# A Fourier mixing layer feeding eight experts: one half store ahead of the sums of weights, the last two batches' early stages 1 to 2 blocks sooner, and the second product of seven from block 40

## The chip, the cores and the metric

The kernel runs on one core of one Trainium2 chip. A core has a matrix engine (TensorE, "PE" in the profile, with its weight loads as "PEld"), VectorE ("DVE"), ScalarE ("ACT"), GpSimd ("POOL") and SyncE ("SP"), which run at the same time and wait for each other through semaphores. Transfers between the chip's memory and the core are issued by SyncE, ScalarE and GpSimd and share 16 DMA engines. The metric is the device time of one execution in microseconds, as the median of several runs.

## The reference

```python
# 1: mixing, per batch and channel: x is (8, 2496, 256)
X = np.fft.rfft(x, axis=1)
Y = X * (filt_r + 1j * filt_i)[None]
x = np.fft.irfft(Y, n=2496, axis=1).reshape(19968, 256)
# 2: each token goes to one of 8 experts by a hash of its id
expert_idx = token_ids * np.int64(2654435761) % np.int64(8)
for e in range(8):                       # w1: (8, 256, 1024), w2: (8, 1024, 256)
    mask = expert_idx == e
    out[mask] = np.maximum(x[mask] @ w1[e], 0.0) @ w2[e]
```

All data are float32.

## The kernel before

**The transform.** A batch of 2496 positions is treated as 39 by 64. `stage1` multiplies with a table of the short transform, and its results go out to a table `d` in the chip's memory. `load2` reads them back turned (`mid<-d` in the profile, L306). `forward` is the second product (`pb`), followed on VectorE by the multiplication with the filter: a product `y`, two halves of a product `z`, and their sum (L321, L325, L326). `back` is the way back (`pc`, L338), written to memory again; `load4` reads it (L409), and `stage3` makes the result (`pd`). The result rows go by indirect transfers of GpSimd (`scatter`, L436) to `xs`, sorted by expert. A full piece of stage 3 issues four such transfers.

**The experts.** `xs` is cut into tiles of 256 tokens of one expert. The main loop takes one tile per step; a step is called a block below, and there are 80 of them that are always needed, numbered from 0. A block has two matrix products, `x @ w1` (`up`) and `h @ w2` (`down`). `up` is made by Strassen's scheme: seven products of halves in place of eight, each of four 128x128x128 matmuls (in float32 each shows as two records). For it, `token_parts` turns the tokens (L861), `token_sums` makes four sums of quarters of the tokens on VectorE (L874), and `weight_sums` makes four sums of quarters of `w1` on GpSimd (L883, tiles `tw`), one block ahead. Inside `up`, VectorE adds products up out of the matrix engine's result memory (L900), and ScalarE applies the relu (L897).

**Early and late blocks.** In blocks below `WS` (L54), `down` is a plain product of 16 matmuls of 256 columns (L928). From block `WS` on, `late_step` calls `both`, where `down` too is made of seven products (L955). This needs sums of quarters of `w2`. They are made once for each expert by `prepare` (loads L211, four subtractions on GpSimd L199, a write to memory L218), and are loaded with each change of expert into the space of the tables `d_t` and `e_t` (L472). These tables and the filter, whose space holds the tokens' sums in late blocks, are needed by `forward` and `back` until batch 7 has passed them. So `WS` cannot come before the end of batch 7's stage 2.

**The order.** All engines take their instructions in the order in which the program issues them. That order is written out by hand: a list `todo` holds the pieces of batches 2 to 7 with a due time in units of blocks, and `run_until` issues what is due at six places of a block: after `up`, after each of the first three quarters of `down`, and at its end. `batch(b, t1, t2, t3)` spreads six pieces of stage 1 over the interval t1, ten of `forward` and `back` over t2, and six of stage 3 over t3; loads are issued up to 2.5 blocks ahead. `within` moves each piece into the second half of its block.

**Weights and stores.** `weights(i, 0)` and `weights(i, 1)` load `w1` (L467) and `w2` (L470) of block i two blocks ahead, on SyncE's queue, and only where the expert changes; there are two buffers. The result of block i is copied to `osb` (L933) and written by `store`, two indirect transfers of GpSimd, one for each half of 128 tokens (L1021). In an early step the order on GpSimd is: four sums of the next block's weights, both half stores of the block before, and then the scatters of the pieces that fall into the block. In a late step it is: the second half store, the four sums, the first half store.

**Stages of tiles.** Tiles that hold only tokens of the first batches come first: the tiles from block 50 on need all eight batches.

Of the kernel before, what the change touches and what calls it, by code (L numbers as in the profile page):

```python
# [50 lines left out]
NPAD = NT * TB - N  # L51
NQP = NPAD // P
NSURE = NT - 5
WS = 42  # L54

# [68 lines left out]
def kernel(  # L126
# [76 lines left out]
    def prepare(e, part):  # L203

        if part == 0:
            p = t4pool if e < 4 else xpool
            raw[e] = p.tile([P, FP, C], F32, name=f"raw_{e}", tag="t4" if e < 4 else "x")
            w = raw[e][:].rearrange("p k c -> p (k c)").rearrange("p (k f c) -> p k f c", k=4, c=P)
            src = moe_w2[e].rearrange("(fp p) c -> p fp c", p=P)
            for k, (f, c) in enumerate(((0, 0), (1, 1), (0, 1), (1, 0))):  # L210
                nc.sync.dma_start(out=w[:, k], in_=src[:, 4 * f:4 * f + 4, P * c:P * c + P])  # L211
        elif part < 5:
            w = raw[e][:].rearrange("p k c -> p (k c)").rearrange("p (k f c) -> p k f c", k=4, c=P)
            to, p, q = ((0, 2, 0), (2, 1, 2), (1, 1, 0), (3, 3, 1))[part - 1]
            minus(nc.gpsimd, w[:, to], w[:, p], w[:, q])
        else:
            w = raw[e][:].rearrange("p k c -> p (k c)").rearrange("p (k n) -> p k n", k=4)
            nc.sync.dma_start(out=t2_dram[e].rearrange("p (k n) -> p k n", k=4), in_=w)  # L218
# [230 lines left out]
    def weights(i, which):  # L449
# [19 lines left out]
        else:  # L469
            eng.dma_start(out=ws[i][1], in_=moe_w2[bass.ds(e, 1)].rearrange("one (fp p) d -> p (one fp) d", p=P), **kw)  # L470
            if WS <= i < NSURE:
                eng.dma_start(out=late["t2"][i % 2].rearrange("p k f c -> p (k f c)"),  # L472
                              in_=t2_dram[bass.ds(e, 1)].rearrange("one p k -> p (one k)"), **(kw if i >= WS + 2 else {}))

# [251 lines left out]
    def spaced(t0, t1, n):  # L726
        return [t0 + (t1 - t0) * u / n for u in range(n)]

    def within(todo, share=.5):

        return [(t // 1 + .5 + t % 1 * share, piece) for t, piece in todo if t is not None]

    def part1(b, at, loads):
        bt = batches[b]
        return within([(at[u], lambda u=u: bt.stage1(u)) for u in range(NU)] +
                      [(loads[v], lambda v=v: bt.load1(v)) for v in range(NV)])

    def part2(b, at, loads, lag):
        bt = batches[b]
        return (within([(at[u], lambda u=u: bt.forward(u)) for u in range(NS // 2)], .3) +  # L740
                within([(at[u] + lag, lambda u=u: bt.back(u)) for u in range(NS // 2)] +
                       [(loads[g], lambda g=g: bt.load2(g)) for g in range(NS // SG)]))

    def part3(b, at, loads):
        bt = batches[b]
        return within([(at[u], lambda u=u: bt.stage3(u)) for u in range(NU)] +
                      [(loads[v], lambda v=v: bt.load4(v)) for v in range(NV)])
# [53 lines left out]
    todo = [(t - 200, piece) for t, piece in head]  # L801
    todo += [(t, lambda k=k: pads(k)) for k, t in enumerate((10.9, 11.6, 11.9, 16.9, 17.6, 17.95, 22.9))]

    def batch(b, t1, t2, t3):

        a1, a2, a3 = spaced(*t1, NU), spaced(*t2, N_2), spaced(*t3, NU)
        x0, d0, e0 = t1[0] - 2.5, t2[0] - 1.2, t3[0] - 1.2
        out = part2(b, a2, [max(d0, a2[2 * g] - 2.2) for g in range(NS // SG)], .6)
        out += part3(b, a3, [max(e0, a3[2 * v] - 2.2) for v in range(NV)])
        if b > 2:  # L810
            out += part1(b, a1, [max(x0, a1[2 * v] - 2.5) for v in range(NV)])
        return out
# [5 lines left out]
    todo += part2(3, spaced(6.4, 10, N_2), [5.2, 5.4, 5.6, 6.5, 7.5], .6)  # L818
    todo += part3(3, spaced(12, 16, NU), [11.2, 11.4, 12.5])
    todo += batch(4, (7.5, 11), (12.4, 16.4), (18.3, 22.3)) + batch(5, (13, 17), (18.4, 21.6), (23.2, 26.8))  # L820
    todo += batch(6, (20, 24), (25.5, 31.5), (33.6, 39.6)) + batch(7, (28.5, 33), (34, 38.8), (40.6, 46.6))
    for e in range(E):
        t = 26.4 + 1.2 * e if e < 4 else 33.4 + 1.3 * (e - 4)
        todo += within([(t + d, lambda e=e, k=k: prepare(e, k)) for k, d in enumerate((0, 1.1, 1.3, 1.5, 1.7, 1.9))])
    todo.sort(key=lambda t: t[0])
    pre = [t for t in todo if t[0] < 0]
# [31 lines left out]
    def token_parts(i, to=None):  # L858

        xt = work.tile([P, DP, 2, P], F32, name=f"xt_{i}", tag="xt")[:] if to is None else to  # L860
        nc.vector.transpose(out=xt.rearrange("p d h (a t) -> p (h a) d t", t=32),  # L861
                            in_=xg[i][:, :, 0:C // 4].rearrange("p a (c d) -> p a d c", d=DP))
        parts[i] = {(h, d): xt[:, d, h, :] for h in range(2) for d in range(DP)}
# [13 lines left out]
    def weight_sums(i, eng=None):  # L877

        eng, w1, h = eng or nc.gpsimd, ws[i][0], F // 2
        b11, b12, b21, b22 = [w1[:, d, f * h:f * h + h] for d in range(DP) for f in range(2)]  # L880
        t = [tpool[i % 2].tile([P, h], F32, name=f"tw_{i}_{k}", tag=f"tw{k}") for k in range(4)]
        for k, (p, q) in enumerate(((b12, b11), (b22, t[0][:]), (b22, b12), (b21, t[1][:]))):
            eng.tensor_tensor(t[k][:], p, q, op=OP.subtract)  # L883
        sums[i] = t

    def up(i, ht, between=lambda: None):
        w1, x, st, t = ws[i][0], parts[i], parts[i]["sums"], sums[i]
        ps = {k: banks[k].tile([P, 4, P], F32, name=f"up_{i}_{k}", tag=k) for k in "abc"}
        h11, h12, h21, h22 = [ht[:, h, 4 * f:4 * f + 4, :] for h in range(2) for f in range(2)]

        def product(bank, w, xx, first, fs=range(4)):
            for f in fs:
                nc.tensor.matmul(out=ps[bank][:, f, :], lhsT=w[:, f * P:(f + 1) * P], rhs=xx,  # L893
                                 start=first and f == 0, stop=True, skip_group_check=True)

        def relu(out, in_):
            nc.scalar.activation(out=out, in_=in_, func=AF.Relu)  # L897

        def plus(out, bank, other):
            nc.vector.tensor_tensor(out, ps[bank][:], other, op=OP.add)  # L900

        h = F // 2
        product("a", w1[:, 0, 0:h], x[0, 0], True)
        nc.scalar.copy(out=h21, in_=ps["a"][:])
        between()
        product("b", t[1], st[:, 1, :], True)
        plus(h12, "b", h21)
        product("c", t[0], st[:, 0, :], True)
        plus(h22, "c", h21)
        product("a", w1[:, 1, 0:h], x[0, 1], False, (0, 1))  # L910
        product("b", t[2], st[:, 2, :], False)
        plus(h22, "b", h22)
        relu(h22, h22)
        product("a", w1[:, 1, 0:h], x[0, 1], False, (2, 3))
        relu(h11, ps["a"][:])
        product("c", w1[:, 1, h:], st[:, 3, :], False)
        plus(h12, "c", h12)
        relu(h12, h12)
        product("b", t[3], x[1, 1], False)
        plus(h21, "b", h21)  # L920
        relu(h21, h21)
# [96 lines left out]
    def store(i, halves=range(2)):  # L1018
        o = rows[i]
        for h in halves:  # L1020
            st = nc.gpsimd.indirect_dma_start(  # L1021
                out=out[:], out_offset=bass.IndirectOffsetOnAxis(ap=to_rows[i][:, h:h + 1], axis=0),
                in_=o[:, h, :], in_offset=None, bounds_check=N - 1, oob_is_err=False)
            tc.declare_no_dep(st.ins, group="out_rows", reason="distinct rows")
            tc.add_to_no_dep_group("out_rows", st.ins)
# [9 lines left out]
    def ask(i, sooner=False):  # L1035

        j = asked[0]
        if j <= i + 2 or (sooner and j == i + 3 < NT and stage_of[j] == stage_of[j - 1]):
            if j < NT:
                load(j)  # L1040
                asked[0] += 1
# [11 lines left out]
    def late_step(i):  # L1053
        ht = work.tile([P, 2, FP, P], F32, name=f"ht_{i}", tag="ht")
        store(i - 1, (1,))
        if i + 1 < NSURE:
            weight_sums(i + 1)
        store(i - 1, (0,))
        both(i, ht)

    def step(i):
        if i >= WS:
            late_step(i)
            return
        ht = work.tile([P, 2, FP, P], F32, name=f"ht_{i}", tag="ht")
        if i + 1 < NSURE:
            weight_sums(i + 1)
        if i > 0:
            store(i - 1)
        up(i, ht, lambda: ask(i))  # L1070
        weights(i + 2, 0)
        if i + 1 < NSURE:
            token_parts(i + 1)
            token_sums(i + 1)
        run_until(i + .6)
        down(i, ht, lambda k: spot(i, k))
        weights(i + 2, 1)
        run_until(i + 1)
# [59 lines left out]
```

## Time and profile before

| | us |
|---|---|
| median of 3 runs (1409.99 to 1411.53) | 1410.83 |
| the profiled execution | 1449.27 |
| its span, from the first to the last instruction | 1447.6 |
| TensorE busy | 1381.2 |
| VectorE busy | 884.7 |
| GpSimd busy | 831.2 |
| ScalarE busy | 418.5 |
| mean granted clock of TensorE, as a share of full speed | 0.984 |

The profiled execution is one run with the hardware profiler on. Its time is 38.4 us above the median of the plain runs. A row of the profile names a line of the kernel, an engine, an operation, and the tile that is written and those that are read; `x8` counts instructions. In a timeline a row has its start and its duration in us, and in brackets how long its engine had been idle before it and what ended that. In a table of stretches each engine has its busy time and, in brackets, its instructions; then follow the clock, the mean busy share of the DMA engines, and the GB/s that they moved. In a list of waits, a row has the time in total, the number of times, and the longest.

### The profile page before, as it was taken

How to read it: one execution, taken by the hardware profiler on the slowest of the kernel's cores; microseconds unless marked ns; L12 is line 12 of the kernel's file. 1: busy time of each engine (PE TensorE's matmuls, PEld its weight loads, DVE VectorE, ACT ScalarE, POOL GpSimd, SP SyncE). 2: the span in 40 equal slices, each digit the busy share in tenths (PEclk: the TensorE clock that was granted, in tenths of full speed). 3: DMA queues.
4: the chain of work that ended last, by engine and by line, in shares of the span. 5: the costliest groups of instructions: out<-in, count | busy, mean ns of one | idle time of the engine just before them, and what ended most of it. 6: DMA issues, size and time to landing. Idle time of an engine off the chain costs nothing.

```text
span 1447.6 us, 26942 instructions
## 1 busy us (share of the span) xinstructions
PE 1381.2 (95%) x9618; PEld 1282.0 (89%) x9618; DVE 884.7 (61%) x1708; ACT 418.5 (29%) x776; POOL 831.2 (57%) x736
## 2 busy tenths in 40 slices
PE   7887999899999989999999999999999999999997
PEld 7775888788888878888899988999999999999997
DVE  6673485465466446534765577456776667677775
ACT  4543222232223222323222222222222222222222
POOL 6155342753475464557766378777565555555663
PEclk9998999999999999999999999999999999999999
DMA  8675765658897597698997876766662616161611
GB/s 221 203 239 182 197 206 144 193 192 257 264 263 251 161 292 225 216 280 258 292 298 219 234 225 214 202 221 194 219 190 48 212 45 215 40 212 45 215 46 34
DMA packets 253949, 284.67 MB, mean 197 GB/s; under 512 B 125651, under 2 KB 222342, under 8 KB 243620
## 3 DMA queue, kind: packets, MB, share of 16 engines
q1 hardware_dynamic: 104589, 185.62, 41.0%
q10 hardware_dynamic: 129303, 52.69, 15.2%
q0 software_dynamic: 19920, 44.59, 8.9%
q8 instruction: 79, 1.29, 0.4%
q14 instruction: 58, 0.48, 0.1%
HBM read 302.04 MB, written 86.15 MB: 268 GB/s over the span
## 4 chain that ended last, share of the span: by engine, by line
PE 83%; DMA 6%; DVE 6%; another core or an unknown queue 2%; issue 1%; ACT 1%; ACTq 0%; SPq 0%; POOLq 0%; DVEq 0%; POOL 0%
PE dps L928 19%; PE up_b L893 8%; PE up_a L893 5%; PE dnc L955 4%; PE pd L270 4%; PE dna L955 4%; PE dnb L955 4%; PE up_c L893 4%; PE upc L950 4%; PE upa L950 4%; PE pb L315 4%; PE pa L270 3%; PE pc L338 3%; DMA xg<-xs 3%; PE upb L950 2%; PE dne L955 2%
## 5 line engine op out<-in xcount | busy, mean ns | idle before, releaser
L928 PE MATMUL dps<-wts,ht 128*128 128x256 f32 x1344 | 314.1, 382 | 0.2 <-ACT ht L897 0.2
L436 POOL DMA_INDIRECT xs<-o,sidx x176 | 178.6, 1015 | 212.5 <-ACT o L272 82.7
L1021 POOL DMA_INDIRECT out_dram<-osb,no x158 | 167.0, 1057 | 221.1 <-DVE osb L962 162.5
L928 PEld LDWEIGHTS dps<-wts,ht 128*128 128x128 f32 x1344 | 255.8, 192 | 38.8 <-issue 2.4
L883 POOL TENSOR_TENSOR tw<-wts 128x512 f32<-128x512 f32 x158 | 203.7, 1289 | 87.3 <-DMA wts<-in_moe_w_dram 61.2
L883 POOL TENSOR_TENSOR tw<-wts,tw 128x512 f32<-128x512 f32 x158 | 204.4, 1294 | 6.2
L900 DVE TENSOR_TENSOR ht<-up_b,ht 128x512 f32<-128x512 f32 x126 | 87.1, 691 | 124.2 <-PE up_b L893 69.6
L897 ACT ACTIVATE ht<-ht 128x512 f32<-128x512 f32 x126 | 79.2, 630 | 176.5 <-DVE ht L900 151.2
L325 DVE TENSOR_TENSOR z<-pb,filt 64x512 f32<-64x512 f32 x160 | 110.2, 689 | 27.6 <-PE pc L338 24.2
L959 ACT ACTIVATE ht<-ht 128x512 f32<-128x512 f32 x114 | 71.9, 631 | 154.3 <-DVE ht L962 106.5
L933 DVE COPY osb<-dps 128x512 f32<-128x512 f32 x42 | 29.1, 692 | 127.2 <-PE dps L928 113.8
L893 PE MATMUL up_a<-xt,wts 128*128 128x128 f32 x672 | 96.7, 277 | 4.6 <-issue 1.9
L893 PE MATMUL up_b<-st,tw 128*128 128x128 f32 x672 | 90.7, 278 | 6.7 <-DVE ht L900 5.1
L893 PEld LDWEIGHTS up_a<-xt,wts 128*128 128x128 f32 x672 | 88.7, 192 | 7.8 <-issue 3.3
L893 PEld LDWEIGHTS up_b<-st,tw 128*128 128x128 f32 x672 | 82.5, 193 | 9.0 <-POOL tw L883 5.1
L341 ACT COPY mid<-pc 128x512 f32<-128x512 f32 x60 | 34.9, 582 | 167.2 <-PE pc L338 69.1
L955 PE MATMUL dna<-wts,ht 128*128 128x128 f32 x608 | 80.4, 275 | 0.0
L900 DVE TENSOR_TENSOR ht<-up_c,ht 128x512 f32<-128x512 f32 x84 | 57.9, 689 | 36.0 <-PE up_c L893 22.0
L270 PE MATMUL pd<-t,wi_t 120*117 120x256 f32 x320 | 77.1, 383 | 2.2 <-ACT o L272 1.3
L950 PE MATMUL upa<-filt,wts 128*128 128x128 f32 x592 | 78.2, 275 | 0.0
L315 PE MATMUL pb<-mid,d_t 128*128 128x256 f32 x280 | 74.9, 391 | 3.0 <-DVE z L325 1.9
L321 DVE TENSOR_TENSOR y<-pb,filt 128x512 f32<-128x512 f32 x80 | 55.1, 688 | 36.1 <-PE pb L315 27.6
(209 smaller groups left out, 2613.8 us busy)
## 6 DMA issues: line engine op xcount, KB each, us to landing
wts<-in_moe_w_dram SPq DMA_DIRECT2D x162, 1024.0 KB
xg<-xs ACTq DMA_DIRECT2D x321, 64.0 KB
d_t<-t2s SPq DMA_DIRECT2D x19, 1024.0 KB
e_t<-t2s SPq DMA_DIRECT2D x19, 1024.0 KB
mid<-d SPq DMA_DIRECT2D x70, 256.0 KB
d<-mid ACTq DMA_DIRECT2D x60, 256.0 KB
x<-in_x_dram SPq DMA_DIRECT2D x39, 312.0 KB
t<-d SPq DMA_DIRECT2D x12, 960.0 KB
```

Of the source, the lines that this page charges most:

```text
L270: nc.tensor.matmul(out=ps[0:cols * H, k, :], lhsT=w[:], rhs=src[:, 2 * i + k, :], start=True, stop=True)
L315: nc.tensor.matmul(out=ps[:, i, :], lhsT=d_t[:, s, :], rhs=rhs, start=True, stop=True)
L325: nc.vector.tensor_tensor(out=z[b], in0=ps[a], in1=f_t[1][64 * hi:64 * hi + 64, s1:s1 + 2, :], op=OP.mult)
L436: st = nc.gpsimd.indirect_dma_start(out=xs[:], out_offset=bass.IndirectOffsetOnAxis(ap=index, axis=0), in_=rows, in_offset=None, bounds_ch ...
L883: eng.tensor_tensor(t[k][:], p, q, op=OP.subtract)
L893: nc.tensor.matmul(out=ps[bank][:, f, :], lhsT=w[:, f * P:(f + 1) * P], rhs=xx, start=first and f == 0, stop=True, skip_group_check=True)
L897: nc.scalar.activation(out=out, in_=in_, func=AF.Relu)
L900: nc.vector.tensor_tensor(out, ps[bank][:], other, op=OP.add)
L928: nc.tensor.matmul(out=ps[:, h, :], lhsT=ht[:, h, fp, :], rhs=w2[:, fp, :], start=(fp == 0), stop=(fp == FP - 1))
L950: nc.tensor.matmul(out=ps[:, f, :], lhsT=w[:, f * P:(f + 1) * P], rhs=xx, start=first and f == 0, stop=True, skip_group_check=True)
L955: nc.tensor.matmul(out=ps[:, 0, :], lhsT=a[:, f, :], rhs=b[:, f, :], start=first and f == 0, stop=True, skip_group_check=True)
L1021: st = nc.gpsimd.indirect_dma_start(out=out[:], out_offset=bass.IndirectOffsetOnAxis(ap=to_rows[i][:, h:h + 1], axis=0), in_=o[:, h, :], i ...
```

## The change

Three edits. `WS` goes from 42 to 40, so that blocks 40 and 41 make their second product of seven too. The due times of batches 6 and 7, and of the preparation of the sums of `w2` of experts 4 to 7, are moved: batch 6's stage 1 half a block earlier, its stage 2 one block earlier and over 5 blocks in place of 6, its stage 3 one block earlier; batch 7's stage 1 and 2 and the preparation two blocks earlier, its stage 3 1.2 blocks earlier. In an early step, the second half store of the block before is issued ahead of the sums of weights, and the first half after them, as in a late step.

```diff
-WS = 42
+WS = 40
...
-    todo += batch(6, (20, 24), (25.5, 31.5), (33.6, 39.6)) + batch(7, (28.5, 33), (34, 38.8), (40.6, 46.6))
+    todo += batch(6, (19.5, 23.5), (24.5, 29.5), (32.6, 38.4)) + batch(7, (26.5, 31), (32, 36.6), (39.4, 45.4))
     for e in range(E):
-        t = 26.4 + 1.2 * e if e < 4 else 33.4 + 1.3 * (e - 4)
+        t = 26.4 + 1.2 * e if e < 4 else 31.4 + 1.3 * (e - 4)
         todo += within([(t + d, lambda e=e, k=k: prepare(e, k)) for k, d in enumerate((0, 1.1, 1.3, 1.5, 1.7, 1.9))])
...
         ht = work.tile([P, 2, FP, P], F32, name=f"ht_{i}", tag="ht")
+        if i > 0:
+            store(i - 1, (1,))
         if i + 1 < NSURE:
             weight_sums(i + 1)
         if i > 0:
-            store(i - 1)
+            store(i - 1, (0,))
```

## The prediction

> **What bounds the kernel now.** I read the page first, then TensorE's waits, then a cut of the span into blocks (a block begins with the first matmul of its first product), then the timeline of two stalls.
>
> ```profile
> span 1447.6 us, 26942 instructions
> PE 1381.2 (95%) x9618; PEld 1282.0 (89%) x9618; DVE 884.7 (61%) x1708; ACT 418.5 (29%) x776; POOL 831.2 (57%) x736
> PE 83%; DMA 6%; DVE 6%; another core or an unknown queue 2%; issue 1%; ACT 1%; ACTq 0%; SPq 0%; POOLq 0%; DVEq 0%; POOL 0%
> ```
>
> TensorE is the bound: 95% busy, 83% of the chain that ended last. Time falls only if TensorE gets less work or stands still less. The cut, with us, busy time per engine, clock, DMA share and GB/s:
>
> ```profile
> 910.00:923.60 13.60, 13.50 (x90) 12.48 (x89) 5.02 (x11) 3.55 (x6) 12.87 (x12) 1.00 0.59 193
> 923.60:938.40 14.80, 14.80 (x97) 13.71 (x96) 5.84 (x12) 4.13 (x7) 7.70 (x8) 1.00 1.03 254
> 938.40:953.90 15.50, 15.16 (x97) 13.87 (x97) 5.79 (x12) 4.04 (x7) 10.91 (x11) 1.00 0.60 172
> 953.90:968.90 15.00, 14.47 (x121) 13.99 (x120) 10.21 (x21) 4.46 (x9) 12.39 (x11) 1.00 0.71 228
> 968.90:983.90 15.00, 14.59 (x122) 14.13 (x122) 9.12 (x21) 4.45 (x9) 12.06 (x12) 1.00 0.74 226
> 983.90:998.60 14.70, 14.48 (x122) 14.02 (x121) 8.85 (x21) 4.45 (x9) 11.46 (x11) 1.00 0.50 144
> 998.60:1012.70 14.10, 14.01 (x119) 13.08 (x119) 9.16 (x22) 4.01 (x9) 9.91 (x9) 1.00 0.83 287
> 1012.70:1025.20 12.50, 12.50 (x115) 12.50 (x114) 8.79 (x20) 3.49 (x7) 7.32 (x6) 1.00 0.89 295
> ```
>
> These are blocks 39 to 46. From 42 on they are late blocks (14 products); 40 to 45 each carry a piece of batch 7's stage 3. A bare late block is 12.50, TensorE never idle. The stalls:
>
> ```profile
> PE up_b L893 <- DVE ht L900: 11.5, 13, 3.8
> PE pa L270 <- issue: 6.0, 2, 3.9
> PE pc L338 <- DVE y L326: 4.9, 2, 3.1
> ```
>
> All small, and none is for a DMA. The 4.9 are one of 3.10 in block 1 and this one in block 3 (214.5 to 236.0):
>
> ```profile
> 220.38 1.27 POOL L883 TENSOR_TENSOR tw<-wts 128x512 f32<-128x512 f32 x1 [2.17 <-DMA wts<-in_moe_w_dram]
> ...
> 223.19 1.24 DVE L874 TENSOR_TENSOR st<-st,xt 128x128 f32<-128x128 f32 x1
> 224.36 1.35 DVE L874 TENSOR_TENSOR st<-xt 128x128 f32<-128x128 f32 x1
> 225.63 0.28 DVE L874 TENSOR_TENSOR st<-xt,st 128x128 f32<-128x128 f32 x1
> ...
> 228.79 0.45 PE L338 MATMUL pc<-y,e_t 128*128 128x256 f32 x1 [1.82 <-DVE y L326]
> ```
>
> GpSimd makes block 5's weight sums as soon as the weights are there, at 220.38 to 225.56, beside VectorE's token sums; those take 1.24 and 1.35 in place of 0.28. VectorE is late, y is late, TensorE waits 1.82. A second kind of stall, in block 24 (from 644.7):
>
> ```profile
> 648.80 0.99 POOL L436 DMA_INDIRECT xs<-o,sidx  x1 [0.30 <-issue]
> 649.81 1.27 POOL L883 TENSOR_TENSOR tw<-wts 128x512 f32<-128x512 f32 x1
> 650.70 0.69 DVE L900 TENSOR_TENSOR ht<-up_b,ht 128x512 f32<-128x512 f32 x1 [2.25 <-PE up_c L893]
> 651.54 0.68 PE L893 MATMUL up_b<-xt,tw 128*128 128x128 f32 x4 [1.32 <-DVE ht L900]
> ```
>
> up_b ended at 648.88, yet VectorE was let go 0.89 after GpSimd went from indirect transfers to sums. I call this a hold: a row of indirect transfers that turns straight into sums. It costs when it falls on an addition with little slack.
>
> **Part 1, blocks 40 and 41 late.** Products of four 128-column matmuls start 0.895 apart; a second product in halves is 16 matmuls of 256 columns, 1.73 for four. Early: 7 x 0.895 + 4 x 1.73 = 13.2. Late: 14 x 0.895 = 12.5. Two blocks: 1.3 less. With the stage-3 pieces I use rows: blocks 39 to 45 now are 13.6 + 14.8 + 15.5 + 15.0 + 15.0 + 14.7 + 14.1 = 102.7. Afterwards the pieces sit one block earlier: block 39 is early with a piece (14.8), 40 to 43 late with one (mean of 15.0, 15.0, 14.7: 14.9 each), 44 the last piece (14.1), 45 bare (12.5): 101.0. **Gain 1.7**, or 1.3 if every late piece costs 15.0. SyncE issues two more 1 MB loads of sums (0.33 each); each has a block of 14.8 to land while TensorE works. If that cover were gone, TensorE would wait for the rest of the landing.
>
> **Part 2, the half store.** It changes GpSimd's order in each early block: half store (1.0, and 0.3 between two), four sums (5.2), half store. Where GpSimd is ahead, the sums can no longer begin in the block before; the store waits for osb (mostly ready 0.9 to 1.2 into the block), so sums run from about 2.4 to 7.6, under additions out of PSUM. Token sums start at 7.8. What waits behind the store is the sums and then the scatters; the sums' reader is TensorE in the next block, at least 4 us after they would end in every early block. In block 3 the 2.6 us of collision go and with them **1.8**. Block 1's 3.10 stays: there the sums wait for the weights till 176.4, store or not. A lone store ahead of sums gives no hold: bare late blocks do just that, without a stall.
> Where GpSimd is behind with scatters, the sums begin 1.3 later. In blocks 15 and 24 they began 4.6 and 5.1 into the block and held the third addition (stalls 0.86 and 1.32); at 5.9 and 6.4 that addition is past: 2.2 gained. In blocks 11, 17, 18, 23 and 26 they began at 3.7 (stalls 0.6, 0, 0.7, 0.1, 0) and move to 5.0, block 24's place: up to 1.3 each, 6.5 together; but block 12 began at 5.1 without a stall, so I take a little over half, 3.6, less the 1.4 that goes. Net 0.0, between -2.2 and +4.3 - 1.4 = +2.9. Token sums lengthen by up to 1.0 in such blocks; behind them y is ready at least 1.9 us ahead of its product in every block from 7 on, so nothing; without that slack it would be 1.0 a block. Block 6's sums follow ten indirect transfers; one place later may add 1.3 to its stall of 3.81; I take **+0.4** as an expectation.
>
> **Part 3, stages sooner.** TensorE's work is only moved. It costs where cover is thin. Batch 6's third load is now asked for at the end of block 19, ahead of the stage-1 piece in block 20 that frees its buffer; SyncE waits with it some 7 us into block 20, with block 21's second and block 22's first weights behind. Block 20 is 31 long and their readers sit 6 us into block 21 or later: 0. Batch 6's stage 2 moves one block, batch 7's stage 1 two blocks, so blocks 23 to 25 (53.2 us, 14.8 MB by the rows below) take about 2.3 MB more.
>
> ```profile
> 626.30:644.70 18.40, 18.29 (x110) 15.80 (x108) 7.26 (x16) 6.12 (x12) 12.93 (x12) 1.00 1.04 315
> 644.70:661.30 16.60, 15.28 (x97) 13.91 (x96) 5.96 (x11) 4.56 (x8) 13.21 (x13) 1.00 0.93 293
> 661.30:679.50 18.20, 17.74 (x109) 16.07 (x109) 8.63 (x17) 5.09 (x9) 13.95 (x14) 1.00 0.73 229
> ```
>
> Here a rule differs from the row. The Trainium skill (DMA: Bandwidth & Descriptors, Specifications) gives about 358 GB/s of HBM per core: 19.0 MB would fit, all of it hidden. The rows show engines full at about 300: 16.0 MB, so 1.1 MB spill, 4 us. By the page 0; by the row 4 us of lateness against leads of 0.7 block (12 us): also 0. Were that lead gone, 4 us of stall. Stage 3 of batch 6 gains room, its first read comes 1.8 blocks after the last back product in place of 0.9. Counted at 5.2 for four sums and 1.3 for each transfer or subtraction, GpSimd has 85 of 92 us to do in blocks 32 to 36 (94 of 106 in 33 to 38 before); I add **+0.4** for that, between 0 and 2.
>
> **Price of a new stall.** The Trainium skill (TensorE: Matmul & The Clock Gate, What's actually happening) halves the clock after an idle window of about 3.4 us; shorter stalls would cost face value. The trace is harsher: block 1's 3.10 is followed by 184.5 to 189.2 at 0.64, block 20's 0.36 + 1.89 by a mean of 0.95 over 31.2 us. 1.82 in block 3 left 1.00. So block 3 is worth 1.8 by both, a new 4 us stall 4 by the page and 5.7 by the rows (3.4 us at half lose 1.7); I use the rows.
>
> **Sum.** -1.7 - 1.8 + 0.0 + 0.4 + 0.4 = -2.7; the profiled execution (1449.3, of it 1447.6 span and 1.7 around it) would become 1446.6. The runs without profile stand at 1410.8, 38.4 shorter; the removed pieces are TensorE time and engine order, so I carry them over whole: **1408.1**.
>
> **Rivals.**
> A. Only TensorE's saving survives: holds arrive in all five blocks, or block 3's stall finds another cause. For it: the four places at exactly 5.0. Against: blocks 5 and 12. -1.7 + 1.2: about 1410.3.
> B. Slower by the hold: one more transfer before the sums lengthens the standstills of block 6 (1.87 + 3.81, clock 0.87) and block 19 (2.40 + 1.84, clock 0.88). Each 1.3 longer may open another half-clock window, 3.0 each; with the five new holds (+5.1) and without the other gains but 1.7, 1410.8 + 9.4 = 1420 at the worst, 1415 at half. It decides once new waits pass 6.3 (the gains of 3.5, and 2.8 for 0.2%). For it: standstills sit at the longest rows of transfers. Against: rows keep their length, only the place of one store changes.
> C. DMA crowding in blocks 23 to 25 makes batch 6's first product late: 4 us and half a clock window, 1408 + 5.7 = 1414. Against: TensorE waits for no DMA at a share of 1.04.
> D. The shift breaks up one standstill of block 6 or 19: 5 to 8 less, 1402.
>
> **How the numbers follow.** Chances: main case 0.44 (own range 1405.5 to 1410), A 0.26, B 0.13, C 0.09, D 0.08. 0.2% (2.8 us) is what a measurement can tell: faster means below 1408.0. The main case lies on that edge and gives 0.28 faster, 0.16 same; D 0.08 faster; A 0.26 same; B 0.12 slower, 0.01 same; C slower. Faster 0.36, same 0.43, slower 0.21. Range 1403 to 1414.5: it leaves out most of D and the upper half of B and C.
>
> **What would show it.** Right: blocks 40 and 41 near 14.9; no wait in block 3; sums beginning about 2.4 into blocks GpSimd is ahead in; stalls gone from 15 and 24. Wrong: new up_b waits at 5 us into blocks 11, 17, 18, 23, 26; longer ones in 6 and 19; pb or pd waiting for a DMA after block 23.

## The result, and the profile after

The changed kernel takes 1428.8 us (1427.2 to 1430.8); the kernel before takes 1410.4 beside it (1408.4 to 1411.5). The ratio is 1.0143, with a 95% interval from 1.0117 to 1.0169: **18.4 us slower**. The forecast was 1408.1, in a range of 1403.0 to 1414.5.

The prediction reads a profile of an execution that is much longer than the plain runs. For what follows, the kernel before was profiled again in an execution of 1406.0; it is called "before, plain" here. The page of after, first its lines that answer to those shown of before:

```profile
span 1425.5 us, 27077 instructions
PE 1371.5 (96%) x9666; PEld 1278.0 (90%) x9666; DVE 936.5 (66%) x1726; ACT 421.3 (30%) x780; POOL 832.6 (58%) x736
```

and those of before, plain:

```profile
span 1404.3 us, 26942 instructions
PE 1365.1 (97%) x9618; PEld 1273.2 (91%) x9618; DVE 908.3 (65%) x1708; ACT 420.8 (30%) x776; POOL 833.7 (59%) x736
```

TensorE is the bound in both. VectorE is 28 us busier. Its sums of tokens in early blocks (L874, tile `st`, three groups in the profile) take 133.7 in place of 102.6, though there are eight fewer. The largest of these groups, in after and then in before, plain (behind the bar: busy us, mean ns of one):

```profile
L874 DVE TENSOR_TENSOR st<-xt 128x128 f32<-128x128 f32 x82 | 73.8, 901 | 1.4
L874 DVE TENSOR_TENSOR st<-xt 128x128 f32<-128x128 f32 x86 | 49.9, 580 | 1.5
```

The two more late blocks add work to VectorE too, and the sums `y<-y,z` take 12.8 less. TensorE's waits in after, the longest of them:

```profile
PE pb L315 <- DMA mid<-d: 4.5, 1, 4.5
PE pb L315 <- issue: 4.4, 2, 3.4
...
PE pd L270 <- DVE z L325: 3.0, 3, 1.6
PE pb L315 <- DVE z L325: 3.0, 2, 1.9
PE pc L338 <- DVE z L325: 2.7, 2, 2.6
...
PE pd L270 <- DMA t<-d: 2.5, 2, 1.9
...
PE pa L270 <- DVE z L325: 2.3, 2, 1.9
```

and the waits of before, plain, behind `z` from block 0 on:

```profile
PE pd L270 <- DVE z L325: 1.8, 2, 0.9
...
PE pc L338 <- DVE z L325: 1.3, 1, 1.3
```

The wait of 4.5 for a transfer (`mid<-d`) is new. The waits behind `z` have grown: from block 0 on, they are 3.1 in before, plain, and 9.9 in after (1.1 of the row of `pb` behind `z` lies ahead of block 0), and most of the 4.4 that end with "issue" will turn out to belong to them. To place all this I cut each trace into blocks and took from each block what its matmuls need at full clock: 13.2 for an early one, 12.5 for a late one, 0.43 for each further 256-column matmul of a piece. The rest is called excess (idle time, and time lost to half clock). Sums by stretch, in us, from one execution of each kernel:

| blocks | before, plain | stages moved only | after | after, sums of tokens late | both repairs |
|---|---|---|---|---|---|
| 0 and 1 | 4.7 | 10.2 | 5.7 | 3.5 | 3.4 |
| 2 to 17 | 8.0 | 8.9 | 6.0 | 8.7 | 11.0 |
| 18 to 21 | 2.8 | 12.8 | **16.9** | 9.9 | 5.6 |
| 22 to 26 | 1.3 | 1.6 | 2.4 | 5.3 | 4.8 |
| 27 to 38 | 4.0 | 8.8 | **13.5** | 4.4 | 5.6 |
| 39 to 45 | 1.6 | 0.3 | 0.3 | 0.3 | 0.3 |
| span | 1404.3 | 1423.2 | 1425.5 | 1410.0 | 1409.3 |

Executions of one kernel differ, so only large differences count: another one of the kernel before, the first of the experiments, has 8.3 in blocks 0 and 1 and 11.6 in 18 to 21. The 10.2 of the stages moved in blocks 0 and 1, where nothing is moved, are such a difference.

The loss lies in blocks 18 to 21 (14.1) and 27 to 38 (9.5). Half of the second part (4.8) is there with the stages moved alone. Where the prediction looked for gains, they came: block 3 is 19.2 and has no wait, and blocks 39 to 45 are at bare time. Blocks 39, 40 and 44 of after, as a table of stretches:

```profile
892.60:907.50 14.90, 14.90 (x98) 13.78 (x97) 5.84 (x12) 4.13 (x7) 9.46 (x9) 1.00 0.76 234
907.50:921.70 14.20, 14.20 (x121) 13.93 (x120) 10.82 (x21) 4.45 (x9) 12.42 (x11) 1.00 0.72 234
...
964.40:978.10 13.70, 13.70 (x118) 12.95 (x117) 9.97 (x21) 4.01 (x9) 10.54 (x9) 1.00 0.48 146
```

Late blocks with a piece are 14.2, with TensorE never idle.

**Block 18: a queue's order.** SyncE's issues (SPq) and the first product they feed, in after (block 17 begins at 470.7, block 18 at 483.8):

```profile
476.73 2.52 SPq L252 DMA_DIRECT2D x<-in_x_dram  x3
479.37 0.47 SPq L409 DMA_DIRECT2D t<-d  x1
484.21 10.60 SPq L306 DMA_DIRECT2D mid<-d  x4
...
496.53 1.71 PE L315 MATMUL pb<-mid,d_t 128*128 128x256 f32 x4 [4.55 <-DMA mid<-d]
```

and in before, plain (block 17 begins at 471.2, block 18 at 484.4):

```profile
477.89 2.54 SPq L306 DMA_DIRECT2D mid<-d  x4
...
492.78 1.03 PE L315 MATMUL pb<-mid,d_t 128*128 128x256 f32 x4
...
494.64 6.61 SPq L252 DMA_DIRECT2D x<-in_x_dram  x3
```

Stage 1 of batch 6 is due half a block sooner, and its first load of `x` with it. That load is now issued in block 17 *ahead* of batch 5's reads `mid<-d`, where before it came behind them. SyncE then stands still before its next reads, as its own waits show (470 to 500):

```profile
SPq L306 <- DMA xg<-xs: 8.3, 1, 8.3
SPq L306 <- DMA x<-in_x_dram: 4.3, 1, 4.3
```

The four reads that were all issued by 480.4 are now strung out to 494.8. TensorE waits 4.55, and its granted clock over the block is 0.93: 6.5 in all.

**Block 28: late on VectorE.** In after (the block begins at 695.3):

```profile
702.71 1.00 POOL L1021 DMA_INDIRECT out_dram<-osb,no  x1 [0.15 <-issue]
...
703.08 3.32 DVE L874 TENSOR_TENSOR st<-xt 128x128 f32<-128x128 f32 x1
703.74 3.85 POOL L199 TENSOR_TENSOR raw<-raw 128x512 f32<-128x512 f32 x3
...
706.43 1.30 DVE L874 TENSOR_TENSOR st<-st,xt 128x128 f32<-128x128 f32 x1
...
708.06 0.68 DVE L321 TENSOR_TENSOR y<-pb,filt 128x512 f32<-128x512 f32 x1
708.75 1.39 DVE L325 TENSOR_TENSOR z<-pb,filt 64x512 f32<-64x512 f32 x2
...
710.24 1.10 PE L315 MATMUL pb<-mid,d_t 128*128 128x256 f32 x4 [3.36 <-issue]
```

The first half's store and the preparation's subtractions follow the sums of weights on GpSimd and meet VectorE's four sums of tokens, which take 5.2 in place of 1.1. The `y` and `z` of a product that TensorE finished at 702.6 are queued behind them. Products of pieces share four buffers of result memory (`fps`). The first `pb`, two `pa` and a `pc` fill them, so the next `pb` starts only when `z` has read the first: 3.36 of standstill, ending 0.1 after `z`. The profile calls its releaser "issue"; the times name it.

**Block 32: a read that lands late.** Not every wait in blocks 27 to 38 is one behind `z`. In after:

```profile
779.03 2.60 PE L270 MATMUL pd<-t,wi_t 120*117 120x256 f32 x8 [1.95 <-DMA t<-d]
```

This is a read of batch 6's stage 3, which the change moved too. With half a clock window behind it, the block has an excess of 3.9; before, plain, has no such wait there. With the stages moved alone the wait is 0.66. Why the read is late was not tested.

### The profile page after: what moved, and what is told of

It is laid out like the page before. It is cut to its first block, busy times and chain, and to the rows that moved or that the text cites. A ratio compares the mean times of both kernels' runs of the same rounds, so it can differ in the third digit from the quotient of the medians.

```text
span 1425.5 us, 27077 instructions
## 1 busy us (share of the span) xinstructions
PE 1371.5 (96%) x9666; PEld 1278.0 (90%) x9666; DVE 936.5 (66%) x1726; ACT 421.3 (30%) x780; POOL 832.6 (58%) x736
## 5 line engine op out<-in xcount | busy, mean ns | idle before, releaser
L928 PE MATMUL dps<-wts,ht 128*128 128x256 f32 x1280 | 297.7, 381 | 0.3 <-ACT ht L897 0.3
L928 PEld LDWEIGHTS dps<-wts,ht 128*128 128x128 f32 x1280 | 243.1, 191 | 36.1 <-issue 2.0
L900 DVE TENSOR_TENSOR ht<-up_b,ht 128x512 f32<-128x512 f32 x120 | 82.9, 691 | 97.7 <-PE up_b L893 72.4
L893 PE MATMUL up_a<-xt,wts 128*128 128x128 f32 x640 | 92.9, 279 | 3.5 <-DVE xt L861 3.3
L893 PE MATMUL up_b<-st,tw 128*128 128x128 f32 x640 | 86.2, 278 | 1.3 <-DVE ht L900 0.5
L955 PE MATMUL dna<-wts,ht 128*128 128x128 f32 x640 | 84.5, 275 | 0.0
L950 PE MATMUL upa<-filt,wts 128*128 128x128 f32 x624 | 82.4, 275 | 0.0
L893 PEld LDWEIGHTS up_b<-st,tw 128*128 128x128 f32 x640 | 78.8, 194 | 3.0 <-issue 2.8
L199 DVE TENSOR_TENSOR filt<-ht 128x512 f32<-128x512 f32 x80 | 61.2, 765 | 27.9 <-ACT ht L959 27.9
L955 PEld LDWEIGHTS dna<-wts,ht 128*128 128x128 f32 x640 | 77.9, 192 | 0.0
```

What stands on the lines that cost most here:

```text
L928: nc.tensor.matmul(out=ps[:, h, :], lhsT=ht[:, h, fp, :], rhs=w2[:, fp, :], start=(fp == 0), stop=(fp == FP - 1))
L950: nc.tensor.matmul(out=ps[:, f, :], lhsT=w[:, f * P:(f + 1) * P], rhs=xx, start=first and f == 0, stop=True, skip_group_check=True)
L955: nc.tensor.matmul(out=ps[:, 0, :], lhsT=a[:, f, :], rhs=b[:, f, :], start=first and f == 0, stop=True, skip_group_check=True)
```

## The experiments

Kernels of one group ran on one chip, beside runs of the kernel before. Ratios are to those, with 95% intervals.

**1. The parts one by one.** First the kernel before again, to have its profile near its plain runs:

> The kernel before, unchanged, to have its profile from an execution whose time is near its plain runs. The profile shown before was of an execution of 1449.3, 38.4 longer than the median. Theory 1 (that execution was disturbed at single places): span about 1409, head some 13 shorter (block 0 begins at about 143 in place of 156), and blocks 1, 6 and 19 some 5 to 8 each shorter; then gains counted from that profile in those places were not there to be had. Theory 2 (the profiler lengthens every execution alike): again about 1447, the same stalls at the same places.

It took 1420.0: between the theories. The head (what runs before block 0) was 11.4 shorter and blocks 6 and 19 were at bare time, but blocks 18 and 20 had 4.1 and 5.7 of excess. The kernel before varies by itself in those blocks.

The half store alone (before, with the last hunk of the change):

```diff
+        if i > 0:
+            store(i - 1, (1,))
         if i + 1 < NSURE:
             weight_sums(i + 1)
         if i > 0:
-            store(i - 1)
+            store(i - 1, (0,))
```

> The kernel before with the half store ahead of the sums of weights in early blocks, and nothing else. Theory H (the half store is what costs: the sums wait for osb, the first half's store and the subtractions of the preparation land on VectorE's sums of tokens in blocks 27 to 33, VectorE is late, and TensorE waits for result memory that VectorE has not read): slower than before by 8 to 15 us. Theory M (the moved stages are what costs): within 2 us of before, or 1.8 faster by block 3 (the prediction's own sum for this part: -1.8 + 0.0 + 0.4).

1408.2 beside 1409.2: ratio 0.9987 (0.9974 to 1.0000). So theory H is wrong: alone, the half store costs nothing that can be measured. It brings 2.3 in block 3 and costs 1.1 in block 15, 1.3 in block 21 and 1.1 in block 34.

The moved stages and preparation alone (`WS` stays 42):

> The kernel before with only the stages of batches 6 and 7 and the preparation moved; late blocks still begin at 42, and both half stores stay behind the sums. Theory M (loads of x for batch 6 go ahead of batch 5's reads of d on SyncE's queue, TensorE waits 4.5 in block 18 and runs at half clock behind it; batch 7's pieces crowd blocks 26 to 33): slower than before by 10 to 18. Theory H: slower by 4 to 8 at most, of it block 18 alone (5.3 over the block's bare time), the rest of the loss then being the half store's. The prediction's sum for this part was +0.4.

1422.2 beside 1409.2: ratio 1.0087 (1.0066 to 1.0108). Theory M holds for this part: block 18's excess is 7.0, blocks 27 to 38 have 4.8 more than before, plain.

The changed kernel without the half store:

> The changed kernel with both half stores behind the sums again, so that stages are moved and late blocks begin at 40. Against the run with the stages moved alone it tells what blocks 40 and 41 bring: 1.3 to 4 less (the prediction: 1.7; the trace after: 4.7 over blocks 39 to 45). Theory H: 2 to 5 slower than before, some 14 faster than the changed kernel. Theory M: as slow as the changed kernel or 2 more (block 3's gain gone), 1428 to 1431.

1421.0: ratio 1.0092 (1.0062 to 1.0122). It lies between the theories. Against the run above, blocks 39 to 45 are 98.0 in place of 99.3: **1.3 for two late blocks**, less than the totals can tell apart. Against the changed kernel (1428.8) the half store costs 7.8, or 7.2 by the two ratios, where alone it cost nothing. The two parts don't add up; they meet somewhere.

**2. The order on SyncE.** The stages moved, but batch 6's loads of `x` due 2.0 blocks ahead:

```diff
-            out += part1(b, a1, [max(x0, a1[2 * v] - 2.5) for v in range(NV)])
+            lead = 2 if b == 6 else 2.5
+            out += part1(b, a1, [a1[2 * v] - lead for v in range(NV)])
```

> The kernel with only the stages moved, but the three loads of x for batch 6 are due 2.0 blocks ahead of their pieces in place of 2.5, so that the first of them is issued behind batch 5's first reads of d on SyncE, as in the kernel before. Stage 1 itself stays half a block sooner. Theory Q (the order on SyncE's queue costs: a wait of 5.0 for mid<-d and 1.7 at half clock in block 18, and what follows in 19 and 20): block 18 back to 18.4, the whole 7 to 10 shorter than the run with the stages moved (1422.2), at 1412 to 1415. Theory P (the pieces crowd blocks 18 to 20, whatever the order of the loads): 1420 or more.

Block 18 fell to 18.9, excess 0.6 in place of 7.0, so the order is the cause of its wait. But the whole was 1418.7, ratio 1.0071 (1.0045 to 1.0096): only some 2 to 3 came through, which these intervals don't tell from nothing. Block 20 shows where 3.0 of it went (excess 6.0 in place of 3.0). Its timeline in this run (the block begins at 527.9; the kernel's lines are one further down):

```profile
535.77 1.27 POOL L884 TENSOR_TENSOR tw<-wts 128x512 f32<-128x512 f32 x1 [2.29 <-DMA wts<-in_moe_w_dram]
536.09 1.10 DVE L875 TENSOR_TENSOR st<-xt 128x128 f32<-128x128 f32 x1
...
537.22 1.32 DVE L875 TENSOR_TENSOR st<-st,xt 128x128 f32<-128x128 f32 x1
...
539.74 1.35 DVE L875 TENSOR_TENSOR st<-xt,st 128x128 f32<-128x128 f32 x1
...
546.16 2.00 PE L315 MATMUL pb<-mid,d_t 128*128 128x256 f32 x4 [1.90 <-DVE z L325]
```

The sums of weights now start at 7.8 into the block, when their weights land, and run beside all four sums of tokens, which take 5.1. In before, plain, where block 20 is short (an excess of 0.5), the weights land at 12.5 and the sums of tokens take 1.1. The same collision as in block 28, in a kernel without the half store.

The other way round, before with one number changed, batch 6's stage 1 from 19.5:

> The kernel before with one number changed: batch 6's stage 1 from 19.5 on in place of 20, its loads with it. Nothing else is moved, late blocks begin at 42, no half store. Theory Q: this half block alone costs 7 to 10 (block 18 near 25.3, a wait of 4.5 to 5.0 for mid<-d in it). Theory P: 0 to 2, since only one half block of stage 1 is earlier.

1417.6 beside 1408.2: ratio 1.0071 (1.0047 to 1.0095), block 18 at 25.1 with a wait of 5.0. Half a block for six pieces costs 9 to 10 (the medians, the ratio), as theory Q said. Of that, 6.7 is block 18's excess.

**3. Where the half store hurts, and a first try at something better.** The changed kernel with the half store in blocks 1 to 23 alone:

> The changed kernel with the half store ahead of the sums in blocks 1 to 23 alone; from block 24 on both halves follow the sums. Theory H2 (with the stages moved, the half store pins the sums of weights to 2.2 to 7.3 us into a block and the first half's store to 7.4, on top of VectorE's sums of tokens at 7.8; VectorE is late in blocks 26 to 36 and the matmuls of the pieces wait for result memory): blocks 26 to 36 some 4 shorter, the whole at 1423 to 1425, block 28 near 21.0 and block 32 near 21.0. Rival (the 7.7 between the changed kernel and the one without the half store lie in blocks 15 to 21 or in the head): within 1.5 of the changed kernel, 1427 to 1430.

1424.9: ratio 1.0109 (1.0080 to 1.0138), 3.8 less than the changed kernel, with intervals that overlap. Blocks 26, 28, 29 and 33 lost 4.4 of excess together, block 28 went to 21.8; block 32 stayed at 22.3, against the expectation. Two executions of the changed kernel differ by as much (block 28 is 23.7 and 26.5, block 32 is 22.2 and 20.2), so this run alone shows little.

Before with the half store in blocks 1 to 7 and `WS` at 41:

> The kernel before with the half store ahead of the sums in blocks 1 to 7 alone, and late blocks from 41 on; no stage is moved. If block 3's 2.3 and one late block's 0.67 are what the change has to give, and the half store's costs lie in later blocks (1.1 each in 15, 21 and 34): 2.3 + 0.7 = 3.0 shorter than before, 1406 to 1407. Rival: a load of the sums of the second weights for block 41 has to wait for batch 7's last back product on SyncE and holds the loads behind it: 1410 or more.

1410.1: ratio 1.0010 (0.9996 to 1.0025). The rival's size: block 3 gained 2.3, but blocks 41 and 42 have 3.6 and 0.9 of excess, with a wait of 2.6 in block 41. Its cause isn't the rival's, a late load. In the timeline (the block begins at 894.4):

```profile
903.45 1.69 POOL L883 TENSOR_TENSOR tw<-wts,tw 128x512 f32<-128x512 f32 x1
903.93 1.75 DVE L199 TENSOR_TENSOR filt<-ht 128x512 f32<-128x512 f32 x1
...
909.29 0.27 DVE L962 TENSOR_TENSOR osb<-dnb,filt 128x128 f32<-128x128 f32 x1
909.62 1.16 PE L955 MATMUL dnb<-e_t,filt 128*128 128x128 f32 x8 [2.58 <-DVE osb L962]
```

GpSimd came to its sums of weights only at 902.07, behind four scatters. There they meet the late block's subtractions on VectorE, which take 1.75 where one at 900.49 took 0.69. VectorE reads `dnb` late, and the product that writes it again waits. It is a collision like the one in block 28, this time with GpSimd late. No run tests it.

**4. VectorE's order.** If late sums of tokens are the cause, they can be issued behind the pieces' work instead ("late sums" from here on):

```diff
             token_parts(i + 1)
-            token_sums(i + 1)
         run_until(i + .6)
-        down(i, ht, lambda k: spot(i, k))
+        def quarter(k):
+            spot(i, k)
+            if k == 2 and i + 1 < NSURE:
+                token_sums(i + 1)
+        down(i, ht, quarter)
```

> The changed kernel with one thing more: in early blocks VectorE's four sums of tokens for the next block are issued behind the third quarter of the second product and the pieces due by then, in place of ahead of them. No instruction is added or left out. Theory V (GpSimd's sums of weights and stores lengthen the sums of tokens from 1.1 to as much as 7.3 us, and the y and z of the pieces, queued behind them on VectorE, come late; TensorE then waits for y or for the result memory that z frees): the waits for y and z in blocks 15, 20, 21, 28 and 32 to 36 go, some 10 us, to 1416 to 1420; block 18's wait for mid<-d stays (6.5). Rival (the waits come from the number of pieces in a block, the sums are only by chance beside them): 1426 or more.

> The kernel before with the same one edit: VectorE's sums of tokens behind the third quarter in early blocks, and nothing of the change. Theory V: block 3 at 19.2 in place of 21.5 without a half store, and up to 5.5 in block 20, 1.8 in block 21 and 2 in blocks 35 and 36: 4 to 8 shorter, 1401 to 1405, under both kernels. Rival: sums that late make the next block's second product wait for st; 1410 or more.

> The changed kernel with both repairs: the sums of tokens behind the third quarter, and the loads of x for batch 6 due 2.0 blocks ahead in place of 2.5. If block 18's order on SyncE (6) and VectorE's order (10) are the two causes and add up, this comes to 1408 to 1413, near the kernel before; if it then beats the kernel before with the late sums of tokens, the moved stages are worth their two blocks (1.3). Rival (some of the loss lies in the pieces' places themselves): 1415 or more.

In the group of these three, the kernel before itself takes 1439.7. In their order they take 1452.6 (1.0086, 1.0056 to 1.0116), 1439.1 (0.9999, 0.9979 to 1.0020), 1453.7 (1.0099, 1.0073 to 1.0126). None of the expected times came. TensorE has other waits there; of before with late sums:

```profile
PE up_b L893 <- DVE ht L900: 7.6, 8, 1.8
PE up_b L893 <- DVE st L874: 6.6, 6, 2.6
...
PE up_c L893 <- DVE ht L900: 2.4, 3, 1.1
```

The first and the last are the holds of the prediction. In before, plain, and in after the first of these rows is 0.5, one wait. Holds thus belong to executions of the longer kind, and the profile that the prediction read has them too. The chip alone doesn't make the kind: the record gives this group chip 12, and chip 12 also to the group of part 2, in which the kernel before takes 1408.2. What makes it stays open. Inside the traces late sums did what was said (block 1 from 5.0 to 0.1, block 3 from 2.3 to 0.3, block 20 from 5.1 to 0.6, against the profile shown before), but there they were themselves late for the next block (the 6.6). And with the same late sums, the changed kernel with both repairs is 14.6 behind the kernel before here (1453.7 and 1439.1): in executions of this kind the change costs something that the repairs don't reach. Blocks 22 to 26 have 13.2 of excess in the one and 8.6 in the other; what it is stays open.

So the group was repeated with the changed kernel beside it:

> The changed kernel, unchanged, as the base for the next on the same chip. On a chip where the kernel before takes about 1410: about 1428. On one where it takes about 1440 (where TensorE waits behind rows of indirect transfers): 1450 to 1460, since batch 7's and batch 6's pieces meet in blocks 23 and 24 there (12.8 over bare time in the run with the late sums).

1430.4 beside 1408.8: ratio 1.0146 (1.0119 to 1.0172), the result once more.

> The changed kernel with VectorE's sums of tokens behind the third quarter in early blocks, beside the changed kernel on the same chip. Theory V: on a chip where the kernel before takes about 1410, 8 to 12 shorter than the changed kernel (blocks 20, 21, 28 and 32 to 36 at bare time, block 18's 6.5 staying). On the slower kind, 0 to 5 shorter, since sums that late are late for the next block there. Rival: no gain on either.

**1414.3**, ratio 1.0043 (1.0016 to 1.0069): 16.1 shorter by an order alone. VectorE's busy time falls from 933.9 to 882.4. Block 28 in this run (it begins at 689.4):

```profile
696.84 1.00 POOL L1021 DMA_INDIRECT out_dram<-osb,no  x1
697.10 0.65 DVE L321 TENSOR_TENSOR y<-pb,filt 128x512 f32<-128x512 f32 x1
697.77 1.39 DVE L325 TENSOR_TENSOR z<-pb,filt 64x512 f32<-64x512 f32 x2
697.85 4.21 POOL L199 TENSOR_TENSOR raw<-raw 128x512 f32<-128x512 f32 x3
...
700.85 1.03 PE L315 MATMUL pb<-mid,d_t 128*128 128x256 f32 x4
...
704.66 0.28 DVE L874 TENSOR_TENSOR st<-xt 128x128 f32<-128x128 f32 x1
```

The store and the subtractions run as before; `z` reads result memory undisturbed, TensorE doesn't wait, and a sum of tokens is 0.28 once GpSimd's subtractions are done. Blocks 27 to 38 fall from 13.5 to 4.4. Theory V stands for executions of this kind, and the number of pieces is not the cause.

> The kernel before with the sums of tokens behind the third quarter in blocks 1, 20, 21 and 36 alone, and the half store ahead of the sums of weights in blocks 1 to 3 alone; no stage is moved, late blocks from 42. Theory V, from the excess of those blocks: up to 5.0 in block 1, 2.3 in block 3, 0 to 5.5 in block 20, 1.8 in 21, 1.1 in 36: 6 to 12 shorter than the kernel before on either chip. Rival: under 3 shorter.

1404.0: ratio 0.9968 (0.9951 to 0.9985). **Faster than both kernels**, though by less than the least expected: block 20 had only 0.5 to give (as in before, plain), and block 3 is 23.3, an excess of 4.1 in spite of its half store. In its timeline (it begins at 197.1):

```profile
204.77 0.99 POOL L1021 DMA_INDIRECT out_dram<-osb,no  x1 [0.15 <-issue]
...
205.21 2.02 DVE L874 TENSOR_TENSOR st<-st,xt 128x128 f32<-128x128 f32 x1
205.78 1.29 POOL L883 TENSOR_TENSOR tw<-wts 128x512 f32<-128x512 f32 x1
...
211.76 1.48 PE L338 MATMUL pc<-y,e_t 128*128 128x256 f32 x4 [2.21 <-DVE y L326]
```

Block 4 is the first without the half store, so the sums of weights that its step issues follow block 3's last store at once and land on block 3's sums of tokens. With the half store in blocks 1 to 7 this should go:

> The kernel before with the sums of tokens behind the third quarter in blocks 1, 20, 21 and 36, and the half store ahead of the sums of weights in blocks 1 to 7 in place of 1 to 3. If the half store protects block 3 only as long as block 4 has it too (its second half keeps block 5's sums of weights out of block 3), block 3 is 19.2 in place of 23.3 and the whole 3 to 5 shorter than with blocks 1 to 3, at 1399 to 1402. Rival: block 3's loss came from something else, and the whole stays at 1403 to 1405.

In this run's group the kernel before is of the longer kind again: 1431.5 beside 1441.2, **ratio 0.9930 (0.9910 to 0.9951)**. Block 3 is 19.2. So it is the half store of the *next* block that protects a block, and late sums in few blocks pay in both kinds of execution.

> The kernel before, unchanged, for a profile on the same chip as the three others. On a chip where it takes about 1410, no wait behind indirect transfers (up_b waiting for ht under 1 in total); on one where it takes about 1440, some 10 of them and excesses of 7 to 8 in blocks 6 and 19.

1406.0, no holds: the "before, plain" of this text.

**5. Both repairs together.**

> The changed kernel with both repairs, once more: the sums of tokens behind the third quarter in early blocks, and the loads of x for batch 6 due 2.0 blocks ahead in place of 2.5. On a chip where the kernel before takes about 1409: the changed kernel with late sums stood at 1414.3 with 6.1 left in block 18, so 1408 to 1410 if the two causes add up and hold all of the loss. Rival: 1413 or more, part of the loss lying in the moved pieces themselves.

**1408.0** beside 1408.5: ratio 1.0001 (0.9989 to 1.0012). The two repairs take the whole loss away. That they are its only causes does not follow: late sums also remove excess that the kernel before has (block 3, for one), and the kernel before with late sums everywhere was not run beside it in executions of this kind.

> The same, but with the late sums in blocks 1, 15, 19 to 21 and from 26 on alone, since late sums cost 1.5 in block 9 and 3.1 in block 23. Theory: 3 to 5 shorter than with late sums everywhere, 1403 to 1406, under the kernel before. Rival: no shorter than 1408.

**1403.2**: ratio 0.9958 (0.9945 to 0.9971), faster than both kernels. Late sums in four blocks alone gave 0.9968, no different by these intervals, so whether the moved stages are worth anything of their own stays open.

## Why the prediction was wrong

- **Part 1** was right. Forecast 1.7, or 1.3 by bare matmul times; the runs with and without it show 1.3. Late blocks with a piece are 14.2, not the 14.9 of the shown rows, because the rows of 14.7 to 15.0 held waits of 0.1 to 0.5 of that execution.
- **Part 2, block 3**: right, 2.3 in place of 1.8 (the wait, and 0.5 of matmuls that took longer around it). **The holds in 15, 24, 11, 17, 18, 23 and 26** ("Net 0.0, between -2.2 and [...] +2.9") had nothing to act on: in the executions of 1402 to 1431, `up_b` waits for `ht` 0.5 at most. Whether the half store moves them as worked out, in executions that have them, was not run.
- **Part 2, "y is ready at least 1.9 us ahead of its product in every block from 7 on, so nothing"** is the step that failed for the half store's share of blocks 27 to 38, 4.7 of the 9.5. Two things were wrong in it. The size: "up to 1.0" was the lengthening by one more sum of weights; the *second* half of the move, the other store with the preparation's subtractions behind it, was never costed against the sums of tokens. The prediction had both times: it ends the sums of weights at about 7.6, where that store follows (7.4 in block 28), and starts the sums of tokens at 7.8. The four sums of tokens became 5.2 in block 28. And the path: lateness was followed to the product that reads `y`, not to the next product that needs the buffer which `z` has yet to read. The buffer's slack ran out first. Blocks 19 to 21 show the same path: they have 8.1 more than before, plain, with waits of 1.88, 1.90 and 2.56 behind `z`, and late sums take 6.8 of it away.
- **Part 3, SyncE: "0"** is the step that failed for block 18. Of the moved loads of batch 6 it weighed the third, in blocks 19 and 20. The first passes batch 5's reads in block 17, and what is queued behind it there is `mid<-d`, wanted one block later. It measured 6.5 in block 18 in after, and 9 to 10 for that half block alone.
- **Part 3, "I add +0.4 for that, between 0 and 2"**, the price of a fuller GpSimd, is the term that was too small. With the stages moved and no half store, blocks 27 to 38 already have 4.8 more than before, plain. The prediction added up GpSimd's time over five blocks; what costs is where its work falls within a block, beside which work of VectorE.
- **Part 3, the DMA engines: 0** was right for the blocks it spoke of. No wait for a DMA in blocks 23 to 25, though their engines are as full as in the rows shown before. But the load was overestimated: these blocks move 15.3 MB, 0.5 more than in the rows before and not 2.3, so the question in which its rule and its row differ was not put to the test. A full stretch reached 331, so 300 was no ceiling. The sign "`pb` or `pd` waiting for a DMA after block 23" did come, in block 32, where no term of the prediction looked. Blocks 23 to 25 of after:

```profile
603.50:620.30 16.80, 16.80 (x105) 15.35 (x105) 6.90 (x15) 3.73 (x8) 8.97 (x8) 1.00 1.01 281
620.30:636.30 16.00, 16.00 (x102) 14.63 (x101) 9.14 (x15) 5.88 (x11) 12.72 (x13) 1.00 1.00 331
636.30:656.40 20.10, 20.10 (x122) 18.29 (x121) 14.48 (x21) 6.27 (x11) 16.96 (x16) 1.00 0.84 265
```

- **The price of a stall** (4 us of wait cost 5.7 by the rows) held in block 18: 4.55 of idle time cost 6.5. "4 by the page" did not follow even from the figure that the prediction quotes beside it, since 4 is longer than 3.4. But no fixed price holds. In after, 0.65 and 1.90 of waits in block 20 were followed by 3.41 at half clock, and 3.36 in block 28 by none; in the second execution of the changed kernel the same 3.36 came with 6.83 at half clock, and the block took 26.5 in place of 23.7.
- **The rivals.** B ended on the right side by the wrong mechanism, so by luck: holds in blocks 6 and 19, where after has an excess of 0 and of 2.2, the latter behind `z`. C had a product late for a DMA, which came, but through the order of issue and not through full engines, and to batch 5, not 6. A and D spoke of holds and standstills that the plain runs don't have.
- **The sum** took the parts as independent. They weren't: the half store is worth -1.0 without the moved stages and some +7 to +8 with them. The traces show one place where they meet, block 28: moved pieces and subtractions put more work on VectorE and GpSimd where the half store pins the sums. That this makes up the whole difference is not shown; without the half store from block 24 on, 3.8 of it went.

## What to carry to other kernels

When a load is due sooner, list every instruction that it passes on its queue, for its first issue as well as its last, and ask who wants those and when. When work moves on one engine, lay the whole new sequence of that engine beside the other engine's sequence in the same microseconds, with what comes after the moved piece too, and follow lateness to every buffer that the late instruction frees, not only to its reader. And a profile of an execution that is 2.7% off the plain runs must not be mined for gains of 1 us: get one that is near them first.

## What the runs showed that was not expected

- VectorE's 0.28 sum of a 128x128 tile, known from before to take 1.24 to 1.35 beside one of GpSimd's sums, took 2.0 to 3.3 when GpSimd went from an indirect transfer into sums or subtractions meanwhile.
- The same program takes 1408 to 1409 in some groups of runs and 1440 to 1441 in others (medians of the kernel before), with chip 12 on record for one of each. An execution of the longer kind (before, with late sums) has waits behind rows of indirect transfers, 7.6 in 8 places where before, plain, has 0.5 in one, and excesses of 7.0 and 7.6 in blocks 6 and 19 where before, plain, has none.
- Block 20 of the kernel before is 26.7 in one execution and 31.8 in another. In the short one the weights land 4.3 after the sums of tokens begin, when these are done; in the long one 0.6 ahead of them, and the two kinds of sums run side by side.
- A wait's length alone does not settle whether half clock follows: 3.36 in the same place went both ways in two executions of one kernel.
